# One core, slot attention into a soft mixture of experts: larger DMA packets for q and the first-layer weights, scores in 32x32 tiles, and a new ranking of the attention steps

## The chip, the cores and the metric

The kernel runs on 1 core of one Trainium2 chip. The metric is the device time of one execution in microseconds (us); the time given for the kernel is the median of its runs. Engines carry the names of the profile: PE (TensorE; PEld is its weight load), DVE (VectorE), ACT (ScalarE), POOL (GpSimd) and SP (SyncE, which here only issues DMA transfers). All data are float32.

## The reference: what is computed

```python
a = softmax(phi, axis=2)                       # over the 576 tokens; phi: [8, 8, 576, 32]
k_m = einsum('bhsm,bhsd->bhmd', a, k)          # 32 pooled keys per head, 64 wide
v_m = einsum('bhsm,bhsd->bhmd', a, v)          # 32 pooled values per head
attn = softmax(q @ k_m^T / 8, axis=-1)
x = concat_heads(attn @ v_m)                   # [4608 tokens, 512]
logits = x @ moe_phi                           # [4608, 32]: 8 experts x 4 slots
d = softmax(logits, axis=0)                    # over all 4608 tokens
slot_input = d^T @ x                           # [32, 512]
slot_out[e] = relu(slot_input[e] @ w1[e]) @ w2[e]   # w1: [8, 512, 1024], w2: [8, 1024, 512]
out = softmax(logits, axis=1) @ slot_out       # [4608, 512]
```

q, k, v are 9.44 MB each, phi 4.72 MB, w1 and w2 16.8 MB each, the output 9.44 MB.

## The kernel before, in words

**Who sets the order.** Every step is handed to a planner (`Plan.add`) with its engine, its cost, the tiles that it reads and writes, and a rank (`pri`). `Plan.order` runs a list schedule over the five engines and issues the steps in that order, so each engine works through one fixed list and waits at the head of it. All loads and stores go through SP's one list, in order: a load whose buffer is not free holds back all loads behind it. At most eight transfers are under way at once. The ranks of the attention steps come from the table `AT` (L1105): one entry for the first of the four pairs, one for the middle two, one for the last. The list `FIRST` (L507) sets the order of the first loads.

**Attention stage.** The eight batches go in four pairs. For each batch (class `Batch`, L545) phi, k, v and q are loaded (`load`, L500 to L502) with 9 tokens of a head on a partition: a 1152-byte run of phi, a 2304-byte run of q, k or v. Then, per batch:

- `shifted`: the maximum of phi over tokens (DVE L606, PE L614, DVE L621, PE L630, ACT L641), the subtraction (POOL L648), the exponential (ACT L657).
- `summed`: the sums (POOL L669, PE L679) and their reciprocals (DVE L687, L688).
- `pooled` (L692): the pooled keys and values, 72 matmuls in tiles of 64x32 (PE L704), scaled on the way out of PSUM (ACT L721 for keys, L728 for values). The keys are written twice, as blocks of a zeroed tile, so that after the turn a 64x64 weight is block-diagonal: each half of the tokens (`r`) meets its own copy.
- `turned` (L738): keys and values turned on PE (four L748, one L755) and copied out (ACT L762, L771), and the values times `moe_phi` (PE L781, ACT L794).
- `turn_q`: q turned in 32x32 squares (DVE L591, two per batch).

Then, for each of the four chunks (two heads) of the pair: `scores` (L805: 8 matmuls in 64x64 tiles, PE L813, then DVE L827), `softmax` (L834: DVE L843, POOL L848, ACT L853, DVE L858, ACT L863, DVE L867, POOL L871, DVE L874) and `logits` (L877: PE L882). Per pair follow `weigh` and `route` (L892, L994: the softmax over tokens and its product with the attention weights, PE L1010, L1046, L1054, DVE L1065, PE L1085). The last pair uses `weigh_last`; the merge of the four pairs ends in DVE L1233, which writes `SIM`, the slots' input.

**Memory.** One area `arena` of 44288 words per partition holds all attention buffers (`stack`, `place`, L423) and, where these lie no longer or never lay, the 1 MB weight tiles `ws` of 2048 words each. A weight tile can be loaded as soon as the attention buffers under it have been used for the last time.

**Expert stage.** `expert_in` (L1344, PE L1353) multiplies the slots by w1, two 1 MB tiles per expert, each read in two runs of 4096 bytes per partition; `expert_out` and `tail_out` (L1422, L1441, PE L1413) multiply by w2: 11 tiles of 1 MB in 8192-byte runs, then the last five tiles as 20 loads of 256 KB in 1024-byte runs, all of the left half (`d` = 0) of the columns first, so that the left half of the output can begin earlier. `slot_sums` (PE L1325) finishes one half of `slot_out`. `slots` (L1467) makes the combine weights and turns them (PE L1497, L1523; ACT L1504, L1535 to L1539).

**Output.** PE L1578 and L1594, copies out of PSUM on ACT L1570 and DVE L1571, stores from SP at L1607: 14 of 128 or 384 KB in runs of 1024 bytes, then three of 768, 1536 and 2304 KB.

L520 and L1399 are matmuls on ones that keep PE busy while it waits for something.

## Time and profile before

| | |
|---|---|
| median of 3 runs (lowest, highest) | 202.70 us (202.66, 220.46) |
| the profiled execution | 202.39 us |
| its span, first to last instruction | 200.6 us |
| mean granted TensorE clock | 0.973 |
| moved by DMA | 76.47 MB in 34090 packets, 381 GB/s over the span |
| busy: PE, DVE, ACT, POOL | 86%, 67%, 35%, 42% of the span |
| SP issues the last q, `SIM` is written, SP is done issuing stores | at 89.5, 136.7, 191.9 us |

The profile's page gives busy time by engine, forty slices of the span with the busy share of each engine and the rate of the DMA, the chain of work that ended last, and the costliest groups of instructions. From the trace further views can be asked for: who waited for whom, a timeline of one engine, and tables of any stretches of the span. "x" before a number counts instructions; a float32 matmul shows as two records on PE, so that 8 matmuls are "x16".

### The profile page before, as it was taken

How to read it: one execution, taken by the hardware profiler on the slowest of the kernel's cores; microseconds unless marked ns; L12 is line 12 of the kernel's file. 1: busy time of each engine (PE TensorE's matmuls, PEld its weight loads, DVE VectorE, ACT ScalarE, POOL GpSimd, SP SyncE). 2: the span in 40 equal slices, each digit the busy share in tenths (PEclk: the TensorE clock that was granted, in tenths of full speed). 3: DMA queues.
4: the chain of work that ended last, by engine and by line, in shares of the span. 5: the costliest groups of instructions: out<-in, count | busy, mean ns of one | idle time of the engine just before them, and what ended most of it. 6: DMA issues, size and time to landing. Idle time of an engine off the chain costs nothing.

```text
span 200.6 us, 6083 instructions
## 1 busy us (share of the span) xinstructions
PE 172.5 (86%) x2623; PEld 111.0 (55%) x2623; DVE 134.4 (67%) x243; ACT 70.3 (35%) x188; POOL 84.3 (42%) x84
## 2 busy tenths in 40 slices
PE   7999748978699899797999789799999999999930
PEld 6777534636457387464665347464655654557520
DVE  6822640799897899999899996478990110558810
ACT  2022314546341755607463252110201123356600
POOL 7199204589992994889964276000000000000000
PEclk9999997899969999999999999999999999999995
DMA  5999999999999999999999999999999999999996
GB/s 201 362 394 395 381 384 389 381 390 379 397 379 390 389 382 396 383 391 398 404 412 401 409 408 411 408 430 418 415 418 421 378 321 329 356 331 312 398 426 279
DMA packets 34090, 76.47 MB, mean 381 GB/s; under 512 B 2064, under 2 KB 15888, under 8 KB 32400
## 3 DMA queue, kind: packets, MB, share of 16 engines
q1 hardware_dynamic: 34064, 76.09, 100.7%
q8 instruction: 20, 0.33, 0.7%
q14 instruction: 6, 0.05, 0.1%
HBM read 66.65 MB, written 9.44 MB: 379 GB/s over the span
## 4 chain that ended last, share of the span: by engine, by line
PE 34%; DMA 26%; DVE 13%; POOL 11%; issue 4%; SPq 4%; ACT 2%; POOLq 1%; DVEq 0%
DMA arena<-in_moe_w_dram 18%; DMA arena<-in_v_dram 8%; PE bank L1594 6%; PE scbank L813 6%; PE kvbank L704 5%; SPq L502 4%; PE bank L882 4%; POOL arena L848 3%; POOL arena L669 3%; POOL arena L648 3%; POOL arena L871 3%; PE bank L1010 2%; DVE arena L606 2%; DVE arena L827 2%; DVE arena L874 2%
## 5 line engine op out<-in xcount | busy, mean ns | idle before, releaser
L648 POOL TENSOR_TENSOR arena<-arena 128x1152 f32<-128x1152 f32 x8 | 21.0, 2633 | 17.6 <-ACT arena L641 15.1
L591 DVE STREAM_TRANSPOSE arena<-top 128x1152 f32<-128x1152 f32 x16 | 21.6, 1355 | 8.4 <-DMA top<-in_q_dram 8.4
L704 PE MATMUL kvbank<-arena 64*32 64x128 f32 x1152 | 21.2, 279 | 6.1 <-issue 2.9
L520 PE MATMUL kvbank<-ones 128*128 128x256 f32 x82 | 23.7, 426 | 2.4 <-ACT arena L728 1.3
L813 PE MATMUL scbank<-arena 64*64 64x288 f32 x256 | 23.8, 445 | 2.2 <-DVE arena L827 2.1
L669 POOL TENSOR_TENSOR arena<-arena 128x128 f32<-128x128 f32 (+2 forms) x32 | 23.4, 732 | 3.2 <-ACT arena L657 1.3
L704 PEld LDWEIGHTS kvbank<-arena 64*32 64x32 f32 x1152 | 16.5, 107 | 10.8 <-issue 5.9
L871 POOL TENSOR_TENSOR arena<-arena,ssm 128x576 f32<-128x576 f32 x16 | 18.3, 1155 | 9.5 <-DVE ssm L867 7.9
L848 POOL TENSOR_TENSOR arena<-arena,smx 128x576 f32<-128x576 f32 x16 | 18.4, 1153 | 7.6 <-DVE smx L843 7.6
L882 PE MATMUL bank<-arena 128*128 128x288 f32 x64 | 18.8, 425 | 1.3 <-DVE arena L874 0.8
L606 DVE TENSOR_REDUCE arena<-arena 128x128 f32<-128x1152 f32 x8 | 17.1, 2148 | 3.7 <-DMA arena<-in_phi_dram 3.6
L520 PEld LDWEIGHTS kvbank<-ones 128*128 128x128 f32 x82 | 15.9, 209 | 6.1 <-ACT arena L728 1.7
L1571 DVE COPY arena<-bank 128x256 f32<-128x256 f32 (+1 forms) x30 | 14.2, 510 | 5.9 <-PE bank L1594 5.8
L827 DVE STREAM_TRANSPOSE arena<-scbank 128x576 f32<-128x576 f32 x16 | 12.2, 765 | 5.4 <-PE scbank L813 5.4
L1594 PE MATMUL bank<-sr,cT 64*128 64x256 f32 (+1 forms) x104 | 14.7, 355 | 0.7 <-DVE arena L1571 0.6
L813 PEld LDWEIGHTS scbank<-arena 64*64 64x64 f32 x256 | 9.8, 139 | 10.1 <-DVE arena L827 3.6
L853 ACT ACTIVATE arena<-arena 128x576 f32<-128x576 f32 x16 | 11.0, 685 | 11.2 <-POOL arena L848 11.0
L882 PEld LDWEIGHTS bank<-arena 128*128 128x128 f32 x64 | 11.2, 189 | 6.4 <-issue 1.7
L1353 PE MATMUL bank<-arena,SIM 128*32 128x256 f32 x224 | 13.2, 390 | 0.4 <-DVE SIM L1233 0.4
L1594 PEld LDWEIGHTS bank<-sr,cT 64*128 64x128 f32 x104 | 9.9, 185 | 6.4 <-DVE arena L1571 4.6
L1570 ACT COPY arena<-bank 128x256 f32<-128x256 f32 (+1 forms) x24 | 10.3, 445 | 8.4 <-PE bank L1594 7.0
L874 DVE STREAM_TRANSPOSE arena<-arena 128x576 f32<-128x576 f32 x16 | 11.9, 754 | 1.5 <-POOL arena L871 1.5
(139 smaller groups left out, 249.2 us busy)
## 6 DMA issues: line engine op xcount, KB each, us to landing
arena<-in_moe_w_dram SPq DMA_DIRECT2D x25, 1024.0 KB, 14.5
top<-in_q_dram SPq DMA_DIRECT2D x8, 1152.0 KB, 12.6
arena<-in_k_dram SPq DMA_DIRECT2D x8, 1152.0 KB, 10.1
arena<-in_v_dram SPq DMA_DIRECT2D x8, 1152.0 KB, 12.5
arena<-in_moe_w_dram SPq DMA_DIRECT2D x20, 256.0 KB, 6.0
arena<-in_phi_dram SPq DMA_DIRECT2D x8, 576.0 KB, 7.2
out_dram<-arena SPq DMA_DIRECT2D x11, 384.0 KB, 3.4
out_dram<-arena SPq DMA_DIRECT2D x1, 2304.0 KB, 8.1
```

The costliest lines, as they stand in the source:

```text
L520: lambda: nc.tensor.matmul(warm.ap, ones, ones.unsqueeze(1).to_broadcast([P, 2, P]), start=True, stop=True,),
L591: lambda: nc.vector.transpose(qT.ap.rearrange("p (i u y) -> p u i y", i=2, y=Y), qt.ap[:, h * QT_SZ: h * QT_SZ + QT_SZ].rearrange("p (u i ...
L606: lambda: nc.vector.tensor_reduce(mx.ap[:, c0:c1], ph().rearrange("p c j m -> p c m j"), axis=AX.X, op=ALU.max),
L648: lambda: nc.gpsimd.tensor_tensor(ph(), ph(), mb.ap[:, c0:c1].unsqueeze(2).to_broadcast([P, c1 - c0, J, M]), op=ALU.subtract,),
L669: plus = lambda o, x, y: nc.gpsimd.tensor_tensor(o, x, y, op=ALU.add)
L704: nc.tensor.matmul(acc.ap[M * c: M * c + M, a, : 2 * D], ph()[h0: h0 + HALF, c, j, :], kv()[h0: h0 + HALF, :, c, j * D: j * D + D], start= ...
L813: nc.tensor.matmul(scb.ap[HALF * g: HALF * g + HALF, a, :JY], pair[g].kd.ap[h0: h0 + HALF, i, c].rearrange("p r m -> p (r m)"), pair[g].qT ...
L827: lambda: nc.vector.transpose(ex.ap[:, c * PART: (c + 1) * PART].rearrange("p (a x) -> p a x", a=2), scb.ap[:, :, :JY],),
L848: lambda: nc.gpsimd.tensor_tensor(exv(), exv(), bc(mx), op=ALU.subtract),
L871: lambda: nc.gpsimd.tensor_tensor(exv(), exv(), bc(sm), op=ALU.mult),
L882: nc.tensor.matmul(lp.ap[:, :JY], vpb.ap[:, h, :], aT.ap[:, a * JY: (a + 1) * JY], start=(h == 0), stop=(h == H - 1),)
L1594: nc.tensor.matmul(po.ap[:, : x.stop - x.start], cT[bp].ap[y: y + HALF, j // 2 * P: j // 2 * P + P], sr.ap[y: y + HALF, t, x], start=(t == 0),
```

## The change

Eight things are altered at once.

1. **q** is read with 18 tokens per run: 256 runs of 4608 bytes a batch in place of 512 of 2304. Token order inside a batch changes with it; the copies that make the combine weights (`c4`, `cT`) put it right by a permuted access pattern (`by_row`, `by_token`).
2. **w1** tiles are read in one run of 8192 bytes per partition in place of two of 4096. `SIM` is laid out to match, through the last product of `route`.
3. **Scores** run as 16 matmuls in 32x32 tiles per chunk in place of 8 in 64x64: the key tile is no longer block-diagonal, so each half of the tokens has a matmul of its own. The key tile shrinks (two turns in place of four, a 256-column copy in place of 512), its zeroing at the start goes.
4. **The last product of `route`** runs as 16 matmuls of 64 columns in 64x32 tiles in place of 4 of 128 columns in 128x64 tiles, and the masked weights before it are 256 columns wide in place of 512.
5. Together the smaller buffers (`kps`, `kbs`, `wtbs`) leave 2048 words of `arena`: the room of one weight tile.
6. `FIRST`: phi of batch 1 is loaded after the inputs of batch 0; k of batch 1 comes last.
7. `AT` has an entry for each pair, and single ranks for the steps that shared one: maximum, sums, values, the turn of each batch's q, and each chunk's softmax.
8. The planner's rate for 1 MB loads is 419 in place of 412 GB/s, and 44 fill-in matmuls are on offer at the start in place of 40.

```diff
-    KP_W = R * (P + Y)
+    KP_W = P
-    wtbs = stack([2, 2, C, NS], 1)
+    wtbs = stack([2, 2, 2, NS], 1)
-    kbs, vTs = stack([2, C, R, M], 4, fifo=True), stack([C, R, M], 2)
+    kbs, vTs = stack([2, C, M], 4, fifo=True), stack([C, R, M], 2)
-    NWARM = 40
+    NWARM = 44
-        for a in kps.aps:
-            nc.vector.memset(a, 0.0)
-    DMA_RATE, IN_RATE, HALF_RATE, SPREAD = 412e3, 386e3, 350e3, 1.0
+    DMA_RATE, IN_RATE, HALF_RATE, SPREAD = 419e3, 386e3, 350e3, 1.0
-    FIRST = ["phi0.0", "phi1.0", "mphi", "q0.0", "k0.0", "v0.0", "q1.0", "k1.0", "v1.0"]
+    FIRST = [
+        "phi0.0",
+        "mphi",
+        "k0.0",
+        "q0.0",
+        "v0.0",
+        "phi1.0",
+        "v1.0",
+        "q1.0",
+        "k1.0",
+    ]
         def load_q(self, u):
...
-                lambda: qt.ap.rearrange("p (c x) -> p c x", c=C)[:, c0:c1],
-                rows(q, self.b)[:, c0:c1], H * S * D * 4 / self.units,
+                lambda: qt.ap.rearrange("p (t x) -> p t x", t=2),
+                src.rearrange("(t r) x -> r t x", r=P), H * S * D * 4,
...
+        def turned_k(self, u):
...
+                for i in range(2):
+                    nc.tensor.transpose(x[:, i, c0:c1, :], kp.ap[o: o + n, i, :], ii)
...
     def scores(c, pair, ex):
...
-                for a in range(2):
-                    for g in range(2):
-                        h0 = HALF * a
-                        nc.tensor.matmul(
-                            scb.ap[HALF * g: HALF * g + HALF, a, :JY],
...
-                            tile_position=(h0, HALF * g),
+                for r in range(R):
+                    for a in range(2):
+                        for g in range(2):
+                            k, x = HALF * (c % 2) + Y * a, HALF * g + M * r
+                            nc.tensor.matmul(
+                                scb.ap[x: x + M, a, :JY],
+                                pair[g].kd.ap[k: k + Y, i, c],
+                                pair[g].qT[c // 2].ap.rearrange("p (i r x) -> p i r x", i=2, r=R)[
+                                    k: k + Y, i, r, :
+                                ],
...
+                                tile_position=(k, x),
...
     def route(bp, ex, pair, lp):
...
-                    nc.tensor.matmul(
-                        sip.ap[HALF * a: HALF * a + HALF, :P],
-                        pair[g].vm.ap[:, a, :],
-                        wtb.ap[:, g, a].rearrange("p c n -> p (c n)"),
...
+                    for a in range(2):
+                        for y in range(2):
+                            k, x = HALF * y, HALF * y + NS * a
+                            nc.tensor.matmul(
+                                to[x: x + NS, c],
+                                pair[g].vm.ap[k: k + HALF, a, c::2],
+                                wtb.ap[k: k + HALF, g, a],
...
+                                tile_position=(k, x),
     AT = (
         dict(
-            phi=(-1.705, -2.946, -2.863, -1.886),
-            kv=(-0.702, -0.388, -0.807, 0.687),
...
+            phi=(-1.705, -2.946),
+            max=(-1.127, -2.415),
+            kv=(-0.702, -0.388),
+            sum=(6.229, -3.964),
...
-        at = AT[(bp > 0) + (bp == NBP - 1)]
+        at = AT[bp]
...
     def expert_in(e, hb):
-        w1v = w1[e].rearrange("(c p) f -> p c f", p=P)
-        w1b = [load_w(w1v[:, 2 * i: 2 * i + 2], wqs if e == EG else ws) for i in range(2)]
+        w1v = w1[e].rearrange("(y i x z) f -> i y x (z f)", y=2, i=2, z=2)
+        w1b = [load_w(w1v[i], wqs if e == EG else ws) for i in range(2)]
```

The table and `FIRST` say little by themselves; what they do to the engines' lists shows below. In these rows L502 of before and L507 of the change are the loads.

SP's list from the start, before:

```order
L502 DMA arena<-in_phi_dram 128x4x288 x2
L502 DMA arena<-in_moe_phi_dram 128x4x32
L502 DMA top<-in_q_dram 128x4x576
L502 DMA arena<-in_k_dram 128x4x576
L502 DMA arena<-in_v_dram 128x4x576
```

and with the change:

```order
L507 DMA arena<-in_phi_dram 128x4x288
L507 DMA arena<-in_moe_phi_dram 128x4x32
L507 DMA arena<-in_k_dram 128x4x576
L507 DMA top<-in_q_dram 128x2x1152
L507 DMA arena<-in_v_dram 128x4x576
L507 DMA arena<-in_phi_dram 128x4x288
```

The second phi now stands behind the first batch's q, k and v; q's rows are half as many and twice as long.

SP's list around the last inputs of the attention stage, before (from the loads for batch 7, the last one):

```order
L502 DMA arena<-in_phi_dram 128x4x288
L502 DMA arena<-in_k_dram 128x4x576
L502 DMA arena<-in_v_dram 128x4x576
L502 DMA top<-in_q_dram 128x4x576
L502 DMA arena<-in_moe_w_dram 128x2x1024
L502 DMA top<-in_q_dram 128x4x576
L502 DMA arena<-in_moe_w_dram 128x2x1024 x6
```

and with the change:

```order
L507 DMA arena<-in_moe_w_dram 128x1x2048 x2
L507 DMA arena<-in_phi_dram 128x4x288
L507 DMA arena<-in_k_dram 128x4x576
L507 DMA arena<-in_v_dram 128x4x576
L507 DMA top<-in_q_dram 128x2x1152 x2
L507 DMA arena<-in_moe_w_dram 128x1x2048 x7
```

The weight tile that stood between the last two q now goes ahead of phi, so that both q follow each other, and seven weight tiles are behind them.

PE's list where the second batch is pooled and the first chunk is scored (L704 and L720 are the pooling, L748 and L767 the turns of the keys, L813 and L838 the scores), before:

```order
L704 MATMUL kvbank<-arena 32x128 x72
L614 MATMUL bank_62<-ident,arena 128x128
L630 MATMUL bank_64<-ident,pmh_82 64x128 x2
L748 MATMUL bank_63<-ident,arena 128x4x32 x4
L755 MATMUL bank_62<-ident,arena 128x128
L813 MATMUL scbank<-arena 64x288 x8
```

and with the change:

```order
L720 MATMUL kvbank<-arena 32x128 x72
L630 MATMUL bank_64<-ident,arena 128x128
L695 MATMUL bank_62<-maskhp,arena 128x2
L646 MATMUL bank_63<-ident,pmh_83 64x128 x2
L767 MATMUL bank_64<-ident,arena 128x128 x2
L788 MATMUL bank_62<-ident,arena 128x128
L838 MATMUL scbank<-arena 32x288 x16
```

The steps between pooling and scores are the same but for the sums (L695), which now come after the pooling, two turns in place of four, and 16 matmuls of 32 rows in place of 8 of 64. In the listing a row counts matmuls, not records.

More of the change, by code (lines that the diff above doesn't have):

```diff
@@ L436 @@
     maskhp_b = keep("maskhp", [P, 2])
-    maskc_b = keep("maskc", [P, C])
+    maskc_b = keep("maskc", [P, C + 2])
+    maski_b = Tile(ap=maskc_b.ap[:, C:])
     rep_b = keep("rep", [P, 4, NS])
@@ L443 @@
     )
-    NWARM = 40
+    maskc = maskc[:, :C]
+    NWARM = 44
     NTAIL = 3
@@ L470 @@
     add(DVE, 3.0, f, r=[ident_b], w=[maskhp_b, maskc_b, rep_b, ones_b])
+    add(
+        DVE, 0.1,
+        lambda: nc.vector.tensor_tensor(maski_b.ap, maskc[:, :2], maskc[:, 2:], op=ALU.add),
+        r=[maskc_b], w=[maski_b],
+    )
     smxs = sb("smx", [P, U], 2)
@@ new lines, in f @@
+                if y1 == 2:
+                    for a in range(2):
+                        nc.scalar.activation(
+                            vm.ap[o: o + n, a], acc.ap[o: o + n, a, D: 2 * D], AF.Copy,
+                            scale=rs.ap[o: o + n, a: a + 1],
+                        )
+            add(
+                ACT, 2 * (1 - y0) * act(P) + 2 * (y1 - 1) * act(D), f, r=[acc, rs.part(u)],
+                w=[kp.part(u), vm.part(u)][y0:y1],
+            )
+        def turned_k(self, u):
+            kp, kd, n, o = self.kp, self.kd, self.n, u * self.n
+            c0, c1 = u * self.ks, u * self.ks + self.ks
+            tp = b_m.tile()
@@ new lines, in turned_k, with turned_v @@
+            add(PE, (0.27, 4), f, r=[kp.part(u), ident_b], w=[tp], also=[kd])
+            add(
+                ACT, act(2 * n),
+                lambda: nc.scalar.copy(
+                    kd.ap[:, :, c0:c1].rearrange("p i c m -> p i (c m)"),
+                    tp.ap[:, : 2 * C * M].rearrange("p (i c m) -> p i c m", i=2, c=C)[:, :, c0:c1]
+                    .rearrange("p i c m -> p i (c m)"),
+                ),
+                r=[tp], w=[kd.part(u)],
+            )
+        def turned_v(self, u, vpb):
+            vm, vT, n, o, g = self.vm, self.vT, self.n, u * self.n, self.g
+            c0, c1, ks = u * self.ks, u * self.ks + self.ks, self.ks
+            tv, vpp = b_m.tile(), b_m.tile()
+            ii = ident[o: o + n, o: o + n]
@@ L1115 @@
+            pool=(-0.16, -4.115),
+            vals=(6.625, 8.479),
+            q=(-2.516, -1.841),
+            turn=(10.518, 14.159, -1.226, 14.159),
+            chunk=(0.486, 0.971, 4.595, 5.502),
+            soft=(-0.399, 7.494, -0.133, 3.606),
+            logit=(-3.284, -3.805, -9.478, -4.484),
+            route=-7.088,
         ),
         dict(
-            phi=(-3.631, -2.992),
-            kv=(-1.771, -2.348),
-            pool=(-0.774, -0.615),
-            q=(0.409, 1.558),
-            turn=(1.059, 0.998),
@@ L1122 @@
-            chunk=(0.106, 0.219, 0.401, 0.611),
-            logit=(-2.612, -2.214, -1.572, -0.776),
-            route=1.408,
+            phi=(-2.497, -9.685),
+            max=(-10.519, -2.147),
+            kv=(13.047, -4.144),
+            sum=(-8.065, -8.103),
+            pool=(2.266, -0.689),
+            vals=(-3.644, 2.182),
+            q=(-3.443, 0.433),
+            turn=(10.234, 7.74, -2.664, 5.631),
+            chunk=(-0.241, 2.75, 0.047, 3.361),
+            soft=(0.657, -0.708, 3.029, 3.485),
@@ L1125 @@
+            logit=(-7.492, -7.709, -9.311, -9.724),
+            route=3.578,
         ),
         dict(
-            phi=(-0.872, -0.956),
-            kv=(-0.757, -0.522),
-            pool=(-1.049, -0.412),
-            q=(-1.042, -1.118),
-            turn=(-0.279, 0.997),
-            chunk=(0.501, 0.524, -0.903, 1.688),
-            logit=(-0.899, 0.078, -1.255, 0.253),
-            route=1.446,
+            phi=(-1.839, -2.167),
+            max=(-9.484, -9.343),
+            kv=(6.939, 0.534),
@@ new lines @@
+            sum=(0.72, 0.633),
+            pool=(-0.795, 1.868),
+            vals=(-3.689, -0.445),
+            q=(-0.691, -0.233),
+            turn=(4.626, 0.14, 3.255, -2.938),
+            chunk=(-6.742, -4.153, -2.12, -9.294),
+            soft=(-4.746, -1.576, 0.728, 1.498),
+            logit=(-7.578, 1.121, -4.86, 0.959),
+            route=1.623,
+        ),
+        dict(
+            phi=(-2.773, -0.544),
+            max=(-3.506, 7.08),
+            kv=(-2.388, 0.893),
+            sum=(-0.857, -9.528),
+            pool=(-0.774, -0.187),
+            vals=(-3.513, 3.925),
+            q=(5.455, -7.045),
+            turn=(3.191, 6.631, 3.353, 4.218),
+            chunk=(-2.163, -9.47, -7.054, 0.354),
+            soft=(3.773, 6.012, 6.246, 4.843),
+            logit=(-1.358, 1.214, -6.55, -0.745),
+            route=-3.442,
@@ L1147 @@
                 x.load_phi(u)
+                plan.at(bp + at["max"][i], 8)
                 x.shifted(u)
@@ L1503, in slots @@
             add(
-                ACT, act(ND * P), lambda: nc.scalar.copy(c4.ap, t4.ap[:, : ND * P]),
+                ACT, act(ND * P),
+                lambda: nc.scalar.copy(by_token(c4.ap), by_row(t4.ap[:, : ND * P])),
                 r=[t4], w=[c4],
```

129 lines of the change are left out of this document (58 added, 71 removed).

## The prediction

> **What bounds the kernel now.** I read the page first: the span, the DMA's share of it, then the rates.
>
> ```profile
> span 200.6 us, 6083 instructions
> DMA  5999999999999999999999999999999999999996
> ...
> q1 hardware_dynamic: 34064, 76.09, 100.7%
> ```
>
> The DMA engines are busy in every slice from the second to the last but one; their packets fill 100.7% of the span (above 100%, since packets overlap a little). So the time is bytes divided by rate, and the rate differs by stage. A table of stretches (PE, PEld, DVE, ACT and POOL busy, granted clock, DMA share, GB/s), and what three of them moved:
>
> ```profile
> 10.00:22.00 12.00, 9.80 (x181) 7.65 (x180) 4.49 (x7) 3.64 (x7) 11.00 (x10) 1.00 1.05 392
> 36.00:126.00 90.00, 79.65 (x1467) 51.69 (x1467) 81.95 (x129) 41.99 (x117) 66.38 (x61) 0.98 1.05 395
> 100.00:128.00 28.00, 24.85 (x269) 15.66 (x257) 24.18 (x41) 10.48 (x34) 13.70 (x13) 1.00 1.03 408
> 132.00:154.00 22.00, 21.33 (x320) 12.59 (x322) 16.57 (x44) 2.88 (x8) 0.00 (x0) 1.00 1.01 420
> 175.00:185.00 10.00, 9.44 (x78) 6.71 (x74) 6.94 (x18) 5.64 (x16) 0.00 (x0) 1.00 0.95 320
> ```
> ```profile
> DMA packets 2097, 4.70 MB, mean 392 GB/s; under 512 B 63, under 2 KB 63, under 8 KB 2096
> ...
> DMA packets 2954, 11.43 MB, mean 408 GB/s; under 512 B 173, under 2 KB 173, under 8 KB 2950
> ...
> DMA packets 1260, 9.23 MB, mean 420 GB/s; under 512 B 135, under 2 KB 135, under 8 KB 135
> ```
>
> Leave out the packets under 512 bytes: 4.70 MB in 2034 packets is 2304 bytes each (q, k, v), 11.43 MB in 2781 is about 4100 (w1), 9.23 MB in 1125 is about 8200 (w2). Same engines, same queue, three packet sizes: 392, 408, 420 GB/s.
>
> A second thing nearly bounds it. PE's timeline and the chain of work where the experts' first half ends:
>
> ```profile
> 136.37 0.29 DVE L1233 TENSOR_TENSOR SIM<-arena 128x128 f32<-128x128 f32 x1
> ...
> 136.72 7.58 PE L1353 MATMUL bank<-arena,SIM 128*32 128x256 f32 x128 [0.40 <-DVE SIM L1233]
> ...
> 162.75 0.61 PE L1413 MATMUL scbank<-arena 128*32 128x256 f32 x8
> 163.19 0.61 PE L1413 MATMUL kvbank<-arena 128*32 128x256 f32 x8
> ...
> 166.96 1.99 PE L1413 MATMUL kvbank<-arena 128*32 128x256 f32 x16
> 168.88 0.70 PE L1399 MATMUL scbank<-ones 128*128 128x256 f32 x2
> ...
> 162.34 5.93 DMA arena<-in_moe_w_dram
> ```
>
> The last left-half weights, issued at 162.34, are in at 168.3. But PE has worked almost without a gap since `SIM` at 136.7: eight records of such a product take 0.61 us and the next eight may start 0.44 after them (162.75, 163.19), so two take 1.05, and the two at 166.96 took 1.99. PE waited only 0.94 us for these weights. Behind that point a chain through PE and the copies, some 32 us, leads to the end.
>
> **The change, part by part.**
>
> *Packets.* One packet per engine at the rates above takes 2304 x 16 / 392 = 94.0 ns, 4096 x 16 / 408 = 160.6 and 8192 x 16 / 420 = 312.1. Between the last two, 4608 bytes come to 160.6 + 151.5 / 8 = 179.5 ns.
>
> ```profile
> top<-in_q_dram SPq DMA_DIRECT2D x8, 1152.0 KB, 12.6
> arena<-in_moe_w_dram SPq DMA_DIRECT2D x25, 1024.0 KB, 14.5
> ```
>
> q: 4096 packets become 2048, each pair saving 2 x 94.0 - 179.5 = 8.5 ns, over 16 engines 1.09 us. w1 (16 of the 1 MB loads): 4096 become 2048, 2 x 160.6 - 312.1 = 9.1 ns a pair, 1.16 us. Sum **2.25 us**. From below: nothing, if the rate belongs to the stage and not to the packet. From above: packets' own durations are the share times these, 98.7, 165.4 and 315.2 ns (4608: 184.1), and by them the gain is 1.7 + 2.0 = 3.7 us. I take 2.25, the rate by the clock. [...] The windows show 8.5 to 9.1 ns a packet, so here the rows decide unless the stage explains them.
>
> *Scores.* Each record streams 288 columns; records on different tiles run side by side.
>
> ```profile
> 109.93 1.20 PE L813 MATMUL scbank<-arena 64*64 64x288 f32 x16
> ...
> 130.48 1.67 PE L1010 MATMUL bank<-arena 64*32 64x288 f32 x36
> L748 PE MATMUL bank<-ident,arena 128*128 128x128 f32 x32 | 5.2, 286 | 1.5 <-ACT arena L721 1.5
> L762 ACT COPY arena<-bank 128x512 f32<-128x512 f32 x8 | 4.6, 581 | 4.3 <-PE bank L748 4.1
> L1024 ACT COPY arena<-bank 128x256 f32<-128x256 f32 x7 | 2.5, 378 | 3.2 <-PE bank L1010 3.2
> ```
>
> Now 16 records on four tiles are four rounds in 1.20 us. L1010 has eight tiles: nine tokens in groups of four, two records each, six rounds in 1.67. A round costs 0.25 to 0.26 us whether four or eight run. The new chunk has 32 records on eight tiles (two row groups, four column groups): four rounds, again **1.2 us, no change**. No row has a tile of 32 rows; should only four run at once, it is eight rounds, 2.2 us (below, the slower rival). The two turns fewer save 8 x 0.3 us of PE, the narrower copy 8 x 0.2 us of ACT.
>
> *The last product of `route`, masked weights, permuted copies.*
>
> ```profile
> L1065 DVE TENSOR_TENSOR arena<-bank,maskc 128x512 f32<-128x512 f32 x4 | 2.7, 672 | 0.8 <-PE bank L1054 0.5 <-ACT arena L1077 0.4
> L926 DVE TENSOR_TENSOR arena<-L,bank 128x288 f32<-128x288 f32 x3 | 1.3, 442 | 0.7 <-ACT arena L933 0.7
> L1085 PE MATMUL bank<-arena 128*64 128x128 f32 x32 | 2.7, 285 | 0.3 <-DVE arena L1065 0.3
> L1535 ACT CAST cT<-bank 128x384 fp32r<-128x384 f32 x4 | 1.9, 481 | 8.9 <-PE bank L1523 8.9
> ```
>
> The mask falls from 0.67 to about 0.42 us, four times; only the last stands before `SIM`. The product took 2.7 / 4 = 0.68 us a pair; 32 records of half the columns take between half and double of it, which moves `SIM` by -0.3 to +0.7 us, taken as nothing. [...] The permuted copies cost at worst their double, 0.5 us each; ACT sits idle 8.9 us before them and `cT` is first used after 171, so that hides them.
>
> *Order.* This term decides whether the packets' gain arrives.
>
> ```profile
> L456 DVE MEMSET arena<- 128x640 f32 x2 | 1.2, 592 | 0.2
> ...
> 4.68 4.19 DVE L606 TENSOR_REDUCE arena<-arena 128x128 f32<-128x1152 f32 x2 [0.57 <-DMA arena<-in_phi_dram]
> ...
> 16.09 2.24 PE L704 MATMUL kvbank<-arena 64*32 64x128 f32 x144 [0.44 <-DMA arena<-in_v_dram]
> ...
> 25.75 1.94 PE L704 MATMUL kvbank<-arena 64*32 64x128 f32 x116 [0.58 <-DMA arena<-in_v_dram]
> 30.57 0.66 PE L704 MATMUL kvbank<-arena 64*32 64x128 f32 x28 [2.88 <-issue]
> ...
> 33.20 2.72 PE L813 MATMUL scbank<-arena 64*64 64x288 f32 x16
> 30.00:35.00 5.00, 3.97 (x51) 2.40 (x53) 0.29 (x1) 2.17 (x7) 2.17 (x1) 0.77 1.06 390
> ...
> 35.98 0.79 DVE L827 STREAM_TRANSPOSE arena<-scbank 128x576 f32<-128x576 f32 x1 [4.09 <-PE scbank L813]
> ```
>
> The zeroing that goes (1.2 us of DVE) is worth nothing: at 4.68 DVE stood waiting for phi. The fill-in matmuls run only where PE waits, and the planner's rate acts through the order alone. With one phi (0.59 MB, 1.5 us) behind the first v, the first pooling starts near 14.6, and its buffers come free as much sooner. The second starts with the last of the same 8.3 MB, near 25.4 (two q at 0.14 us each sooner). Before, it was cut by 2.88 us in which PE waited for nothing the profile shows, and the first chunk then took 2.72 us, not 1.20 (the granted clock is 0.77 there). Without both, pooling takes 2.2 us, the steps up to the scores 2.0 as before, a chunk 1.2: the first DVE transpose comes near 31 in place of 36. With both again it comes at 35.6. From there DVE works 81.95 of 90 us, the same list but for the masks, so a head start is carried on, less what arrival takes back. I take `SIM` **2 us earlier**, bounds 0 and 5; 1.3 are needed (2.25 less PE's 0.94).
>
> On SP the place to watch is the last q:
>
> ```profile
> SPq L502 <- DVE arena L591: 11.0, 3, 5.8
> ...
> 89.51 0.37 SPq L502 DMA_DIRECT2D top<-in_q_dram  x1
> ...
> top<-in_q_dram SPq DMA_DIRECT2D x1, 1152.0 KB, 9.7
> ```
>
> It waits for DVE to turn an older q, and lands 9.7 us after its issue; 3.0 are its own bytes, so 6.7 us of transfers were ahead. With a weight tile (2.6 us) moved ahead of phi, 4.1 are left, and seven weight tiles now queue behind this wait. It costs nothing while DVE is not 4 us late there. The freed 2048 words let one more weight tile in early, which works the same way.
>
> *Sum.* Profiled execution: 202.39 - 2.25 = 200.1, span 200.6 - 2.25 = 198.4. The median stands 0.3 above the profiled execution: 202.7 - 2.25, **200.4 us**.
>
> **The rivals.**
>
> *PE sets the handover.* `SIM` comes no earlier: the left half gains only PE's 0.94 us, 201.8. For it: PE has no other gap from 136.7 to 168.3. Against it: the start above.
>
> *The rate belongs to the stage.* The 392 is measured beside 11.00 of 12 us of POOL, the 420 beside none; if half the difference is that, the gain is 1.1 us, 201.6. Against it: between 100 and 128 POOL works 13.7 of 28 us and DVE 24.2, and w1 still gets 408. [...]
>
> *More than forecast.* By the packets' own durations 3.7 us, and about 1 us more of the holes at 175 to 185 (share 0.95, 320 GB/s) closed by an earlier `SIM`: 198.0. Against it: that stretch waits for copies, which do not change.
>
> *Slower: 32-row tiles run four at a time.* Sixteen chunks then cost 1.0 us more each, 16 us, less 2.4 for turns. PE is free for 10.35 of the 90 us from 36 to 126, so 3 us must show, and up to 13.6 where a score is what is waited for; I take 9. `SIM` 9 later uses up the 0.94 and puts the end 8.1 later: 210.8. It shows from `SIM` 0.9 late and is 2% from 5.0 late. Against it: L1010's eight tiles side by side, with two row groups.
>
> **How the numbers follow.** Forecast 200.4: 0.50. PE handover 201.8: 0.20. Stage rate 201.6: 0.10. More than forecast: 0.11, and I count it as faster. Four tiles: 0.09. The threshold is 2%, about what a measurement of this kernel can tell from no change: 198.65 and 206.75. So faster 0.11, same 0.80, slower 0.09. The range leaves out half of the faster case and the slower one: 198.5 to 203.2, its upper end being a `SIM` 1.5 us late.
>
> **What would show it.** Right: w1's stretch near 420 GB/s, q's packets 4608 bytes; 32 records of a score in about 1.2 us; the first DVE transpose of scores before 35; `SIM` before 135.4; left-half weights in near 166. Wrong: DMA share under 1.0 anywhere from 5 to 155; scores over 1.8 us; `SIM` at 137 or later with PE gapless up to the handover.

## The result

| | before | with the change |
|---|---|---|
| median of the runs, us | 203.2 | 501.4 (499.7 to 503.2, 4 runs) |
| ratio to before | | 2.470, 95% interval 2.456 to 2.484 |
| span of the profiled execution, us | 200.6 | 499.9 |
| bytes moved, mean rate | 76.47 MB, 381 GB/s | 76.52 MB, 153 GB/s |

The kernel is two and a half times slower; 200.4 us was predicted. The median before contains one execution of 220.46 us; ratios and intervals, here and below, use only executions within 1.5% of the fastest of their kernel. From the page of the changed kernel, the rows that were read first before:

```profile
span 499.9 us, 6757 instructions
DMA  8999686814254111111111111111111499474998
GB/s 311 387 363 351 232 194 169 299 55 128 95 185 160 56 56 53 55 53 54 54 53 54 53 53 52 52 53 53 53 53 55 131 235 250 175 286 143 321 333 352
...
q1 hardware_dynamic: 29744, 76.09, 44.4%
...
another core or an unknown queue 41%; PE 26%; DMA 21%; DVE 4%; issue 2%; ACT 2%; POOL 1%; SPq 0%; POOLq 0%; DVEq 0%; ACTq 0%
```

The bytes are the same, and so is the queue. But through 18 slices the engines are one tenth busy and move some 53 GB/s. The same queue in a stretch of nothing but w1, 225 to 375 us:

```profile
DMA packets 987, 7.98 MB, mean 53 GB/s; under 512 B 14, under 2 KB 14, under 8 KB 14
q1 hardware_dynamic: 986, 7.96, 12.6%
```

8192-byte packets, as intended, and 12.6% of 16 engines: the work of **2.0 engines**. The packets' times say the same: exactly two are under way for 97% of this stretch, and one takes 309 ns; before, in the stretch of w2 from 132 to 154 us, 16 or 17 were under way for 98% of it, and one took 312. So no packet is slower; fewer run at a time. Where PE stands meanwhile, in the chain of waits (start, duration, what):

```profile
36.20 2.41 PE scbank L838 x32
...
60.90 27.67 DMA arena<-in_phi_dram
...
106.72 42.60 DMA arena<-in_phi_dram
...
182.63 1.21 PE scbank L838 x32
...
201.94 0.30 DVE SIM L1300
...
221.00 1.94 PE bank L1420 x16
222.94 17.71 another core or an unknown queue
240.69 1.94 PE bank L1420 x16
```

The transfer's end is not tied to its issue here, hence the odd name of the cause: PE works 1.94 us on a weight tile and waits 17.71 for the next. A tile takes 240.69 - 221.00 = 19.7 us; at the 408 GB/s of before a megabyte takes 2.57. For 16 tiles that is 16 x (19.7 - 2.57) = 274 us, most of the 298 by which the kernel is slower. Some of it falls ahead of `SIM`: the first w1 tiles stand on SP between the inputs (one is issued at 47.6 us, two at 93.9), and the chain stands 28 and 43 us for phi loads behind them, so that `SIM` comes at 201.94 in place of 136.4. The chunk of scores at full clock took 1.21 us, as predicted; the one at 36.20 ran at half clock.

### The profile page after: what moved, and what is told of

It reads as the page before. It is cut to its first block, busy times and chain, and to the rows that moved or that the text cites. A ratio compares the mean times of both kernels' runs of the same rounds, so it can differ in the third digit from the quotient of the medians.

```text
span 499.9 us, 6757 instructions
## 1 busy us (share of the span) xinstructions
PE 207.4 (41%) x2961; PEld 120.8 (24%) x2961; DVE 134.6 (27%) x242; ACT 68.1 (14%) x188; POOL 84.7 (17%) x84
## 2 busy tenths in 40 slices
DMA packets 29773, 76.52 MB, mean 153 GB/s; under 512 B 1840, under 2 KB 15664, under 8 KB 26032
## 4 chain that ended last, share of the span: by engine, by line
another core or an unknown queue 41%; PE 26%; DMA 21%; DVE 4%; issue 2%; ACT 2%; POOL 1%; SPq 0%; POOLq 0%; DVEq 0%; ACTq 0%
DMA arena<-in_phi_dram 17%; PE bank L1420 5%; PE scbank L838 5%; DMA arena<-in_moe_w_dram 4%; PE bank L907 2%; PE bank L1670 2%; PE kvbank L720 2%; DVE arena L622 2%; PE kvbank L535 1%; PE kvbank L1480 1%; PE bank L805 1%; PE scbank L1480 1%; PE bank L1035 1%; PE scbank L1466 1%
## 5 line engine op out<-in xcount | busy, mean ns | idle before, releaser
L1420 PE MATMUL bank<-arena,SIM 128*32 128x256 f32 x224 | 21.9, 544 | 131.0 <-DMA arena<-in_moe_w_dram 130.5
L1453 DVE COPY arena<-bank 128x128 f32<-128x128 f32 x2 | 0.6, 292 | 203.4 <-PE bank L1447 203.4
L1420 PEld LDWEIGHTS bank<-arena,SIM 128*32 128x32 f32 x224 | 8.1, 141 | 144.1 <-DMA arena<-in_moe_w_dram 136.3
L1420 PE MATMUL bank<-top,SIM 128*32 128x256 f32 x32 | 3.9, 630 | 74.7 <-DMA top<-in_moe_w_dram 74.7
L838 PE MATMUL scbank<-arena 32*32 32x288 f32 x512 | 27.2, 526 | 2.1 <-issue 1.9
L720 PE MATMUL kvbank<-arena 64*32 64x128 f32 x1152 | 23.2, 301 | 8.0 <-issue 5.4
L907 PE MATMUL bank<-arena 128*128 128x288 f32 x64 | 23.9, 510 | 2.5 <-DVE arena L899 1.5
L630 PE MATMUL bank<-ident,arena 128*128 128x128 f32 x8 | 3.1, 392 | 51.3 <-DVE arena L622 51.0
L896 POOL TENSOR_TENSOR arena<-arena,ssm 128x576 f32<-128x576 f32 x16 | 18.3, 1148 | 26.3 <-DVE prs L703 20.8
L720 PEld LDWEIGHTS kvbank<-arena 64*32 64x32 f32 x1152 | 18.6, 116 | 13.4 <-issue 8.8
L1420 PEld LDWEIGHTS bank<-top,SIM 128*32 128x32 f32 x32 | 1.3, 157 | 76.9 <-issue 59.2
L1480 PE MATMUL kvbank<-arena 128*32 128x256 f32 x128 | 13.4, 505 | 8.0 <-DMA arena<-in_moe_w_dram 8.0
```

The source lines that it names most:

```text
L720: nc.tensor.matmul(acc.ap[M * c: M * c + M, a, y0 * D: y1 * D], ph()[h0: h0 + HALF, c, j, :], kv()[h0: h0 + HALF, y0:y1, c, j * D: j * D + D],
L838: nc.tensor.matmul(scb.ap[x: x + M, a, :JY], pair[g].kd.ap[k: k + Y, i, c], pair[g].qT[c // 2].ap.rearrange("p (i r x) -> p i r x", i=2, r=R)[
L896: lambda: nc.gpsimd.tensor_tensor(exv(), exv(), bc(sm), op=ALU.mult),
L907: nc.tensor.matmul(lp.ap[:, :JY], vpb.ap[:, h, :], aT.ap[:, a * JY: (a + 1) * JY], start=(h == 0), stop=(h == H - 1),)
L1420: nc.tensor.matmul(hb.ap[NS * j: NS * j + NS, :256], SIM.ap[:, 2 * i + c, NS * e: NS * e + NS], wv[:, c, 512 * (j // 2): 512 * (j // 2) + ...
L1480: nc.tensor.matmul(dst[NS * x: NS * x + NS, :HD], hT()[:, 4 * k + 2 * i + j, NS * e: NS * e + NS], wide[:, j, k, d * HD: d * HD + HD], sta ...
```

## Experiments

Theory A: the new w1 pattern, whose slowest dimension has 2 entries (y = 2), lets only 2 engines work on each tile. The 12.6% above agrees, and so do w2's tiles before, whose slowest dimension has 128: 16 or 17 packets under way. Rival: 8192-byte reads of w1 are slow for another reason, or the new order is.

**The change with w1 in two transfers.**

```
-        load(lambda: t.ap, src, 1 << 20, t)
+        add(SP, 0.06, lambda: [nc.sync.dma_start(t.ap[y:y + HALF], src[y // HALF]) for y in (0, HALF)], ...)
```

> The changed kernel with one edit: each 1 MB w1 tile is loaded by two transfers of 64 partitions instead of one whose source has the two halves of the rows as its outermost dimension. Bytes, 8192-byte packets, destination, order of the steps on every engine: unchanged. Theory A (few engines): with the halves outermost, a transfer is spread over only 2 of the 16 DMA engines; with 64 rows outermost it gets all 16. Then w1 moves at about 420 instead of 53 GB/s, the 300 us vanish and what is left is the rest of the change: 198 to 204 us. Theory B (the rows' addresses: rows of two far halves, or 8192-byte runs out of w1, are slow in themselves): the same bytes come from the same addresses, so it stays at 450 to 500 us. Theory C (the order or the 32x32 tiles cost a good part of it): between, 230 us or more, with w1 fast.

245.3 us (238.1 to 247.3). A stretch of w1 (PE, PEld, DVE, ACT, POOL busy, granted clock, DMA share, GB/s):

```profile
140.00:160.00 20.00, 18.53 (x230) 11.78 (x229) 13.19 (x34) 5.11 (x19) 6.13 (x6) 1.00 1.02 232
```

All engines are busy now (DMA share 1.02), and the rate is 232 GB/s, not 53 and not 408. The large step goes with the number of engines, as theory A says; but 198 to 204 us was expected, so a second limit shows behind it.

**The change with w1 as before.**

```
-        w1v = w1[e].rearrange("(y i x z) f -> i y x (z f)", y=2, i=2, z=2)
+        w1v = w1[e].rearrange("(c p) f -> p c f", p=P)
...
```

> The changed kernel with w1 read as before the change: two runs of 4096 bytes per partition, 128 rows outermost. The rows then do not meet the slots' input that belongs to them, so the numbers out are others; work and order are the same. Theory A: 16 engines, w1 at about 408 GB/s, and against the two-halves kernel 1.2 us slower (4096 packets of 160.6 ns instead of 2048 of 312.1): 199 to 205 us. Theory B: as fast as that, since addresses and packets are those of before. Theory C: 230 us or more.

215.6 us (212.6 to 218.9), ratio 1.056 (1.049 to 1.064). So the rest of the change costs some 11 us by itself, where no more than 3 were expected. `SIM` comes at 150.6, 14 us later than before. By stretches, in the same columns:

```profile
36.00:60.00 24.00, 22.17 (x458) 13.43 (x458) 17.33 (x23) 8.63 (x20) 16.74 (x15) 0.71 0.95 346
60.00:84.00 24.00, 19.97 (x449) 12.62 (x449) 18.77 (x31) 11.46 (x30) 18.50 (x17) 0.86 1.03 382
84.00:108.00 24.00, 20.68 (x393) 13.23 (x399) 18.78 (x32) 9.83 (x30) 17.51 (x16) 0.79 1.00 381
108.00:132.00 24.00, 23.30 (x420) 14.55 (x402) 20.06 (x33) 8.23 (x28) 9.77 (x11) 0.78 0.83 314
```

The clock was 0.93 to 1.00 in these stretches before. (This execution took 216.1 us at a mean clock of 0.880; the shortest took 212.6 at 0.916, so part of the low clock is this execution's own.) DVE worked 84.8 of these 96 us before and now works 74.9; and the DMA has holes, the first sign of being wrong that the prediction named.

**Before with only the new w1 pattern** and **before with it in 16 groups.**

```
-        w1v = w1[e].rearrange("(c p) f -> p c f", p=P)
+        w1v = w1[e].rearrange("(y i x z) f -> i y x (z f)", y=2, i=2, z=2)    # and y=16
...
```

> The kernel before with only the w1 loads of the change (halves outermost, 8192-byte runs); the rows of w1 then do not match the slots' input, so the numbers out are others. Theory A: 2 engines, 53 GB/s in the w1 stretch, DMA share 0.13, about 16 x 17 us more: 480 to 510 us. Theory B: the same. Theory C: clearly less than 480 us, since order and tiles are those of before.

> The kernel before with w1 in 8192-byte runs whose source has 16 groups of 8 partitions outermost, instead of 2 groups of 64: also not in one stride, same packets. The rows do not match the slots' input, so the numbers out are others. Theory A: 16 divides the engines' number, so all 16 work: w1 at 420 GB/s and about 1.2 us less than before, 200.5 to 202.5 us, if PE lets it through (only 0.94 us of it if PE sets the handover). Theory B (rows in several far groups are slow): far above 210 us.

With y = 2: 499.1 us (one execution), 52 GB/s at a DMA share of 0.13 from 140 to 160 us. This pattern alone makes 296.7 of the 298 us; the rest of the change hides behind it. With two packets at a time in the change, each as fast as before (309 ns, 312 before), and the same rows of DRAM read by more engines at 232 GB/s, **theory A is shown** for the 2 entries of this pattern. With y = 16: 241.0 us, ratio 1.195 (1.187 to 1.204), all engines busy (share 1.02) at 234 GB/s. The 200.5 to 202.5 us expected was wrong: the half rate of the run with two transfers is here too.

**The tiles of the scores, from both sides.** Theory B of the next two texts says that small tiles hold the granted clock down. In the change with w1 as before, 16 records on 64x64 tiles in place of 32 on 32x32:

```
...
-                                scb.ap[x: x + M, a, :JY],
-                                pair[g].kd.ap[k: k + Y, i, c],
+                            scb.ap[HALF * g: HALF * g + HALF, a, :JY],
+                            pair[g].kd.ap[h0: h0 + HALF, i, c0: c0 + 2].rearrange("p c m -> p (c m)"),
...
```

> The change with the first layer's weights loaded as before (their contraction rows do not match `SIM`), and each chunk of scores issued as before in 16 records on 64x64 tiles (the stationary operand takes two chunks' keys side by side, so the scores are not the reference's); the order of the steps is untouched. It is the run of the change with w1 as before (215.6 us, granted clock 0.71 to 0.86 between 36 and 132 us) with the tile size of the scores alone turned back. Theory B, the 32x32 tiles keep the granted clock down (32 records occupy half as much of the array at a time, and PE is then taken for idle): the clock returns to 0.95 or more after 48 us, `SIM` comes near 138 in place of 150.9, the time is 203 to 205 us. Rival C, the order with singly ranked steps makes PE wait longer, and the clock falls after each wait, whatever the tiles: clock and time as in that run, 214 to 217 us. Both in part: in between, and the next run says how much.

and before, with 32 on 32x32 in place of 16 on 64x64 (the non-zero blocks of the keys alone):

> The kernel before with its chunks of scores issued in 32 records on 32x32 tiles: the zero blocks of the keys are left out, the two non-zero 32x32 blocks of each 64x64 one are issued by themselves (numbers unchanged), and the order, the q packets and the w1 loads are those of before. Theory B: a chunk still takes 1.2 us at full clock, but the granted clock between 36 and 132 us falls from 0.93 to 1.00 towards 0.7 to 0.9, `SIM` comes 8 to 14 us later, the time is 210 to 216 us. Rival C: clock and time as before, 202 to 203.5 us. By my rival of the prediction, four tiles at a time, a chunk would take 2.2 us at full clock.

208.3 us (207.2 to 209.5), ratio 1.029 (1.025 to 1.033), and 212.7 us (211.4 to 214.9), ratio 1.048 (1.043 to 1.053). So the small tiles cost 5.6 us by the ratios in the change's order, where 208.3 lies between the times of the two theories, and 10 in the order of before. There the clock is 0.86 to 1.00 from 36 to 132 us, and what stands out is PE waiting where the profile shows nothing that it waits for ("issue"). These waits (total, times, longest), and PE's timeline at the longest:

```profile
PE kvbank L704 <- issue: 7.5, 5, 2.8
PE scbank L814 <- issue: 4.6, 3, 3.3
```
```profile
39.11 0.67 PE L814 MATMUL scbank<-arena 32*32 32x288 f32 x2
43.09 2.07 PE L814 MATMUL scbank<-arena 32*32 32x288 f32 x30 [3.31 <-issue]
45.08 0.47 PE L614 MATMUL bank<-ident,arena 128*128 128x128 f32 x1
```

DVE stood behind it:

```profile
45.59 0.29 DVE L621 TENSOR_REDUCE pmh<-bank 128x2 f32<-128x128 f32 x1 [4.22 <-PE bank L614]
```

12.1 us of such waits against 3.2 before. PE stopped in the middle of a chunk. In the trace a packet of 16384 bytes of the instruction queue began at 40.71, and PE went on at 43.09, 2.4 us later; before, such a packet began at 28.17 and PE's one long wait of that kind ended at 30.57, 2.4 later too. The planner counts PE's instructions in blocks of 256 (`BLOCK`) and allows one each 6.0 us (`BLOCK_US`). The traces agree with such blocks: 20 of these packets in the run before, with 5246 records of matmuls and weight loads, and 22 in this one, which has 512 more. Theory F: the **number** of PE instructions costs, not the tile. A pooling uses up more than a block (144 records, each with a weight load) in 2.2 us, and a chunk of 32 records now uses 64.

**Before with each score record cut in two by columns**: 32 records on the 64x64 tiles of before, the same products.

```
+            for s in (slice(0, JY // 2), slice(JY // 2, JY)):
...
-                            scb.ap[HALF * g: HALF * g + HALF, a, :JY],
+                                scb.ap[HALF * g: HALF * g + HALF, a, s],
...
```

> The kernel before with each of the 16 records of a chunk of scores cut into two of 144 columns: 32 records as in the change, but on the 64x64 tiles of before, with the same products, streamed columns and occupied part of the array (numbers unchanged; order unchanged). The kernel before with 32 records on 32x32 tiles took 212.7 us, with 12.1 us of PE waits for nothing that the profile shows ('issue'), 2.9 before, and each of these waits ended 2.4 us after a 16384-byte packet of the instruction queue began. Theory F, the number of PE instructions costs: 512 more of them are two more blocks of 256 to be fetched, and PE stands where a block is used up before the next is in: issue waits of 8 us and more, `SIM` near 144 to 147, 209 to 213 us. Rival B, the small tiles themselves cost (a 32x32 tile does not count as activity and the clock stays halved): issue waits near 3 us, half-speed clock as before (6.8 us before the end), 202 to 204 us.

212.6 us (211.4 to 214.1), ratio 1.048 (1.043 to 1.054): the same as with small tiles. **In the order of before theory F holds and B falls.** The waits, and `SIM`:

```profile
PE kvbank L704 <- issue: 7.2, 6, 2.8
PE scbank L814 <- issue: 4.5, 3, 3.0
```
```profile
148.88 0.29 DVE L1234 TENSOR_TENSOR SIM<-arena 128x128 f32<-128x128 f32 x1
```

For the change's own order this is not shown. The same stretches as above, of the 208.3 us run:

```profile
36.00:60.00 24.00, 19.11 (x394) 12.37 (x393) 18.46 (x27) 9.51 (x25) 17.34 (x16) 0.78 1.01 374
60.00:84.00 24.00, 20.09 (x447) 13.62 (x447) 21.35 (x34) 11.27 (x32) 21.18 (x20) 1.00 1.02 375
84.00:108.00 24.00, 20.32 (x437) 13.09 (x438) 20.81 (x35) 11.54 (x34) 19.00 (x18) 0.93 1.04 401
108.00:132.00 24.00, 22.77 (x270) 13.98 (x268) 21.48 (x35) 8.70 (x32) 11.48 (x10) 0.93 1.02 399
```

Its issue waits are 5.5 us, those of the run with w1 as before 6.6, hardly more; but the clock rose from 0.78 to 0.91 over these 96 us. So there the price of the small tiles goes with the clock, and why stays open.

**The order.** The change with w1 and tiles of before took 208.3, 5.8 us above before; its `SIM` came at 141.7. Is that the order? Three runs: all ranks, first loads and the rate of before put into it; before with the new `FIRST` alone (its edit is shown); and that 208.3 run with only the old `FIRST`.

```
-    FIRST = ["phi0.0", "phi1.0", "mphi", "q0.0", "k0.0", "v0.0", "q1.0", "k1.0", "v1.0"]
+    FIRST = ["phi0.0", "mphi", "k0.0", "q0.0", "v0.0", "phi1.0", "v1.0", "q1.0", "k1.0"]
```

> The change with w1 loaded as before and scores on 64x64 tiles (as in the run that took 208.3 us; contraction rows and scores are not the reference's), and with the ranks of the steps, the list of first loads and the planner's rate of the kernel before: the loads then stand on SP in the order of before but for weight tiles that come one place earlier. What is left of the change are the packets of q, the permuted copies, the narrower keys, the masked weights and the last product of the route. Theory C, the order of singly ranked steps costs the 5.8 us that are left: 201 to 203.5 us, `SIM` at 135 to 138. Rival: one of the small edits costs them (the 64 records of the last product, the permuted copies): 206 to 209 us.

> The kernel before with one edit: the list of first loads (`FIRST`) is that of the change (k0, q0, v0, phi1, v1, q1, k1 behind the first phi); the planner works out the rest with the ranks of before, numbers unchanged. My prediction's order term was that this start brings the first pooling near 14.6, the first DVE transpose of scores near 31 in place of 36 and `SIM` 2 us earlier: 201 to 202 us. In the run of the change with w1 and tiles of before the transpose came at 38.5. Theory G, the new start is itself later (the second batch's chain stands behind the first's): the transpose near 37 to 39, `SIM` 2 to 5 us later, 204 to 207 us. Rival H, the start is worth nothing either way: 202 to 203 us, and the 5.8 us that the change keeps with w1 and tiles turned back lie in the ranks behind it or in the small edits.

> The change with w1 as before and scores on 64x64 tiles (208.3 us; contraction rows and scores are not the reference's), with the list of first loads of before and the new ranks kept. Theory G: the first DVE transpose of scores comes at 34 to 36 in place of 38.5 (33.7 in the run with all ranks of before), `SIM` 2 to 5 us earlier, 203 to 206 us. Rival H: 207.5 to 209.5 us. The ranks of the change were made for its own start, so a slower time than 208.3 would say only that start and ranks go together.

215.1 us (214.5 to 215.9), 210.2 (209.7 to 210.7; ratio 1.036, 1.032 to 1.040), 237.2 (236.1 to 238.4). All three are slower than what they started from, and slower than both theories allowed. In the first of the three, SP's loads stand as before, but for weight tiles one place earlier; DVE's list differs from 41 us on, since other costs go into the same planner; SP once waits 14.7 us for DVE. So the ranks, the start and the steps' costs work as a set in these runs, which can't say how much of the 5.8 us is order: **that stays open**. What the second one shows is the start with the ranks of before. Its PE and DVE:

```profile
26.34 1.94 PE L714 MATMUL kvbank<-arena 64*32 64x128 f32 x119 [0.85 <-issue]
32.50 1.08 PE L714 MATMUL kvbank<-arena 64*32 64x128 f32 x25 [4.21 <-issue]
```
```profile
39.49 0.78 DVE L837 STREAM_TRANSPOSE arena<-scbank 128x576 f32<-128x576 f32 x1 [4.81 <-PE scbank L823]
...
144.92 0.29 DVE L1243 TENSOR_TENSOR SIM<-arena 128x128 f32<-128x128 f32 x1
```

The second pooling starts at 26.3, not 25.4; the issue wait in it grows from 2.9 to 4.2 us, the clock is at half for 10 us from 30.8 on, and the first transpose of scores comes at 39.5 in place of 36.0. The prediction had 31.

**The packets by themselves.** Before, with w1 as one contiguous megabyte over 128 partitions; and with that and q in 4608-byte packets:

```
-        w1v = w1[e].rearrange("(c p) f -> p c f", p=P)
+        w1v = w1[e].rearrange("(i p z) f -> p i (z f)", i=2, z=2)
...
```

> The kernel before with each w1 tile as one contiguous megabyte, 8192 bytes to each of 128 partitions: the very pattern in which the w2 tiles are read at 420 GB/s (16 engines, 64 KB to each, engines 64 KB apart). The contraction rows do not match `SIM`. Theory D, the half rate (231 to 244 GB/s) of the two earlier 16-engine versions with 8192-byte runs lies in their patterns (engines that read 128 KB apart, or that write into 64 partitions only): here w1 runs at 415 to 420 GB/s and the 1.16 us of my prediction's w1 term show, 201.3 us. Rival E, the tensor or its place in the program makes 8192-byte reads of w1 slow: 235 GB/s again and about 241 us.

> The kernel before with both kinds of larger packets and nothing else: q as in the change (two runs of 4608 bytes to a partition), w1 as one contiguous megabyte in 8192-byte runs over 128 partitions; neither layout is what the steps behind expect, so the result is not the reference's. My prediction's packets term by itself. By the clock rates of the windows: 202.5 - 2.25 = 200.25 us. By the run with w1 alone (202.0, a gain of 0.5, interval 0 to 1.0) most of w1's 1.16 us does not come through to the end, and q's 1.09 may be lost the same way (`SIM` and PE set the handover): 201.5 us. Rival, nothing arrives: 202.5 us.

202.0 us (201.3 to 203.4), ratio 0.998 (0.995 to 1.000); and 201.2 us (200.4 to 202.5), ratio 0.993 (0.991 to 0.996). The stretch of w1 in the first, where the prediction shows 408 GB/s before:

```profile
100.00:128.00 28.00, 24.65 (x324) 15.88 (x321) 24.98 (x41) 10.79 (x35) 14.87 (x14) 1.00 1.00 414
```

Together 1.3 us arrive of the 2.25 predicted (0.8 to 1.9). For w1 alone the interval reaches no gain. The form of the first with `SIM`'s rows put in the order which these tiles need, in 16 matmuls for each pair's last product in place of 4 (128 records in all in place of 32):

```
...
-                        sip.ap[HALF * a: HALF * a + HALF, :P],
-                        pair[g].vm.ap[:, a, :],
...
+                            to[NS * b: NS * b + NS, z],
+                            pair[g].vm.ap[:, b % 2, z::2],
...
```

> The kernel before with each w1 tile as one contiguous megabyte over 128 partitions, and the last product of the route in 16 records that write the rows of `SIM` in the order which these tiles need (one 32-row piece of the output for each group of 32 partitions), so the output is the reference's. It is the version of the change's w1 edit that spreads over all engines and costs few PE instructions. By the run with the pattern alone (202.0 us, ratio 0.9976, interval 0.9952 to 1.0): 201.7 to 202.3 us. By my prediction's w1 term, 1.16 us: 201.3. Rival: the 96 records more on PE make `SIM` late and take it back, 202.5 to 203 us.

206.2 us (205.6 to 207.0), ratio 1.018 (1.015 to 1.021), later than even the rival's 203. The 96 records more take back far more than the packets give: 4.2 us against the run without them, with 6.5 us of issue waits in place of 3.6, one of 2.6 in the middle of a pooling. No version that computes the whole of the reference beat the kernel before.

**The half rate.** Before with the w2 tiles (420 GB/s) in two transfers of 64 partitions; the same halves to even and odd partitions; and whole tiles by a source pattern of 16 groups of 8 rows:

```
-                lambda t=t: t.ap, w2v[:, i], 1 << 20, t,
+    [nc.sync.dma_start(t.ap[y: y + HALF], s[y: y + HALF]) for y in (0, HALF)]       # halves
...
+    [nc.sync.dma_start(t.ap[y // HALF:: 2], s[y: y + HALF]) for y in (0, HALF)]     # even and odd
...
+                lambda t=t: t.ap, w2v[:, i].rearrange("(x y) f -> y x f", y=16), 1 << 20, t,   # groups
```

> The kernel before with each of its 9 whole w2 tiles loaded by two transfers of 64 partitions in place of one of 128 (same bytes, same 8192-byte packets, numbers unchanged); w1 as before. [...] Rival: halves run at 420 GB/s, 202 to 203.5 us, and the half rate of the earlier version with w1 in two halves has another cause.

> The kernel before with each of its 9 whole w2 tiles loaded by two transfers of 64 partitions, as in the run that took 227.0 us: the same two contiguous halves of a megabyte in DRAM, but one goes to the even and one to the odd partitions, so each transfer writes across all 128 (the rows land in other partitions, the result is not the reference's). Theory D2, the half rate comes from writing into one half of the partitions: 202 to 203.5 us, w2 at 420 GB/s. Rival D3, it comes from the addresses read (each engine's share 32 KB, next to the neighbour's, in place of 64 KB): 225 to 229 us, w2 near 235 GB/s.

> The kernel before with its 11 whole w2 tiles (I counted 9 in the two earlier expectations; it is 11) loaded through a source pattern of 16 groups of 8 rows, in which engine after engine reads neighbouring rows of 8192 bytes (row x 16 + y goes to partition 8 y + x, so the result is not the reference's). In the run with w1 in 16 groups the engines' shares lay 128 KB apart and the rate was 231 to 244 GB/s. [...] Rival D5, it was the distance of 128 KB: w2 stays at 400 to 420 GB/s, 202 to 204 us.

227.0 us (225.3 to 229.7), 259.7 (259.1 to 262.1), 225.1 (223.6 to 228.5). The stretch from 140 to 160, of the run in halves and of the run in groups (410 GB/s before):

```profile
140.00:160.00 20.00, 18.42 (x309) 10.40 (x301) 10.85 (x31) 3.71 (x10) 0.00 (x0) 1.00 1.01 237
```
```profile
140.00:160.00 20.00, 19.75 (x337) 12.19 (x329) 12.31 (x33) 3.72 (x10) 0.00 (x0) 1.00 1.01 242
```

There are 11 of these tiles, not 9 as two of the texts above say. The engines are all busy in both runs (share 1.01), so each packet takes longer. At 235 GB/s 212 to 220 us were expected of the halves, with 9 tiles, and 222 to 230 of the groups. Even and odd gave the longest time, outside both theories: SP waited for PE and DVE between the transfers (`PE bank L1353`: 37.7 us in 6 waits), which I did not foresee and have not explained. While they ran, they ran at full rate, up to 426 GB/s. The same stretch in slices of 0.5 us:

```profile
DMA  0004968995000000065999960000000009799970
GB/s 0 0 0 131 311 279 344 393 393 213 33 0 0 0 0 0 0 131 147 344 426 377 377 279 16 0 0 16 0 0 0 0 0 262 295 410 410 393 311 16
```

and the median 8192-byte packet of that run took 309 ns, 558 in the run in halves, which reads the same addresses in DRAM. So between these two it is the partitions written that count, not the addresses read. The groups of w2 take neighbouring rows by their pattern and got 242 GB/s, so the 128 KB between the groups of w1 are not needed for the half rate. What the runs show: two transfers of 64 neighbouring partitions (232 and 237 GB/s) and 16 groups of 8 (234 and 242) run at little more than half the rate with all engines busy; transfers over 128 partitions in order (414 to 421) or over the even and the odd ones in turn (up to 426) do not. Why, none of them shows. The distances between the engines' shares in the texts above are worked out from the patterns, an estimate; no trace shows which engine reads what.

## Why the prediction was wrong, point by point

- **Packets: the step that failed.** "One packet per engine at the rates above": the rates hold with 16 engines, and I took from the diff that the packets doubled, not how many engines a tile is spread over. The pattern was in the diff. The term was -1.16 us for w1 and measured +296.7; taken out of the change, it gave back 286. With the spread kept, the two packet terms together are right in sign and mis-sized: 1.3 us in place of 2.25. The price of a packet was part of that: at the 414 GB/s that w1 now gets, a packet of 8192 bytes takes 316.6 ns, so a pair saves 4.6 ns and not 9.1, which is 0.6 us for w1. The 312.1 had come from w2's stretch, so part of that saving belonged to the stage, as one rival said. The 2.25 lies outside the measured 0.8 to 1.9.
- **Scores.** 1.2 us for 32 records on eight tiles was right (1.20 and 1.21 at full clock), and the rival of four at a time falls. What failed is "no change": I priced the array's time and not the 512 instructions more (256 records and their weight loads), 10 us in the order of before. The 5.6 us in the change's own order go with the clock, which the term took as full. The row for the first was in my own fence: the 2.88 us in which "PE waited for nothing the profile shows" was this wait, and I carried it on without asking what feeds PE.
- **Last product of `route`.** A pair's 32 records take 0.58 us at full clock in the chain of the run with w1 as before (1.01 at half): inside my bounds by duration. By number, 96 records more cost 4.2 us in the order of before, 2.9 of them as issue waits.
- **Order.** `SIM` 2 us earlier was predicted, 5.3 later came with w1 and tiles of before. There the first pooling began at 15.5 (14.6 predicted), the second at 26.9 (25.4), the first transpose at 38.5 (31). I had bounded this term at nothing from below, because I let the stall either vanish or stay; it grew.
- **The place on SP.** SP's waits for DVE to turn q went from 12.0 to 27.9 us in the change with w1 as before, the longest from 5.8 to 9.1. The 4.1 us of margin did not hold: SP stood from 100.3 to 115.8 us for a pooling on PE and from 116.8 to 123.3 for a turn of q, both with weight tiles next, and the DMA fell to 76 GB/s from 114 to 117.5 and to 223 from 121 to 124. The larger wait, for PE, was not in the prediction.
- **Signs.** Two of the three signs of "wrong" came: shares under 1.0 and `SIM` after 137 (201.9, and 150.6 with w1 as before); the third, scores over 1.8 us, only where the clock was at half. The range of 198.5 to 203.2 held only what the terms could do with the transfers spread as before.

## What to carry to other kernels

Before pricing a transfer by bytes and packet size, write down both access patterns and ask how many engines their slowest dimension feeds (here 2 entries: 2 packets at a time, 53 GB/s) and which partitions are written at one time (here 64, or groups of 8: 232 to 242 GB/s); of the forms tried for w1, one contiguous tile over all 128 partitions alone kept the full rate with 8192-byte packets (414 GB/s). When an edit turns one matmul into several smaller ones, count PE's instructions as well as its columns: where a stretch already shows PE waiting for nothing that the profile shows, more instructions can cost far more than their columns (here 10 us for 512). And a tuned order belongs to the costs it was tuned with: in three runs, half of one and half of the other was slower than either whole.

## What was new of the hardware

- A 1 MB load with 2 as its outermost dimension: 2 packets at a time, 53 GB/s, 19.7 us; with 16 groups of 8 partitions or as two loads of 64 partitions: all 16 engines busy, 232 to 242 GB/s; over 128 partitions, in the 202.0 us run: 414 to 421.
- PE's instructions come in pieces of 16384 bytes (20 for 5246 PE records before, 22 for 5758 with 32 score records) and PE went on 2.3 to 2.7 us after such a packet began, at each issue wait of the two runs with 32 records in the order of before. In that order it is a bound of its own: 512 instructions more cost 10 us. It is not everywhere: the 215.1 us run has 82 matmul records more than before and 1.3 us of issue waits. In all, 3.2 us of issue waits showed even before the change and 12.1 with the records of the scores doubled.
- The granted clock fell to half in pieces of 3.41 us or whole multiples (but for the last one), 47.8 us of them before the last stretch in the change with w1 as before, 23.9 with the tiles turned back too, 6.8 before. Whether these waits of PE or its small tiles bring that on is not settled: in the order of before it was 13.7 with 32 records on small tiles and 20.5 with 32 on the tiles of before.
